# One load for x's tiles 4 to 15, a part of the output projection moved ahead, and score matmuls that share their weights

## The chip, the cores and the metric

The kernel runs on one core of one Trainium2 chip. A core has four engines that compute: TensorE (PE in the profile; its weight loads are listed apart as PEld), VectorE (DVE), ScalarE (ACT) and GpSimd (POOL). SyncE (SP) issues most of the transfers, which 16 DMA engines carry out. Each engine runs its own instructions in order and waits on semaphores for the others. The metric is the device time of one execution in microseconds, as the median of several runs.

## The reference: what is computed

A transformer block for 2048 positions of width 640, with a modulation that depends on a vector c.

```
sa, ca, ga, sb, cb, gb = six rows of  silu(c) @ w_mod
h  = layernorm(x) * (1 + ca) + sa
q  = h @ wq                                  (32 heads of width 128)
p  = softmax(q @ k_cache^T * 128 ** -0.5)     (2048 keys per head)
x  = x + ga * ((p @ v_cache) @ wo)
h  = layernorm(x) * (1 + cb) + sb
u  = gelu(layernorm(h) @ w1), its four column groups shifted by +1, -1, +2, -2 positions
x1 = h + u @ w2
B  = x1 + gelu(layernorm(x1) @ w3) @ w4       (inner width 1728)
out = x + gb * B
```

Tensors are bfloat16; matmuls accumulate in float32.

## The kernel before

Positions are worked in 16 tiles of 128 rows (NQT). A small class, Prog, takes every operation with the keys that it reads and writes, in the order in which the code calls for it, and puts a semaphore wait only where one engine must wait for another or for a transfer. There is no scheduler: the order of the calls is the order on each engine, and the order of the transfers on SP is the order of the calls as well. A transfer whose wait is not yet over holds back everything behind it on SP.

**The start** normalizes x, transposes it to hT, and computes the modulation rows.

**The loop** (L533) runs over 512 steps s, one for each head and tile (NG = 32 * 16), and then on for PVD + LAG = 12 steps that only finish what is under way. A step has two halves of 1024 keys. For each half TensorE computes the scores of tile s (qk, L279: two matmuls of 512 columns with the same QT slice as weights, L286), then half of the value products of the step eight before (pv, L292: eight matmuls of 129 columns, L299), then at most one piece of the next head's projection (q_piece, L237) or four transposes (t_piece, L253). VectorE negates and scales the scores and takes their minimum (L575). ScalarE takes the exponential (L588) into the slot s % 10 of a ring (Pb). Most tiles are then transposed by a DMA from Pb to the ring's second half (transpose, L220; the issue is L222), and two tiles in 16 by TensorE. GpSimd divides by the sums and stores the outputs to a scratch tensor in HBM (norm, L445; L454).

**Around the end of the loop**, SP is given, in this order: the outputs of tiles 0 and 1 as transposing loads in three parts (load_ot, L496, issue L497; parts of 12, 12 and 8 heads, the last at step NG), x's tiles 0 to 3 (load_xt(0), L503, issue L504), the outputs of tiles 2 and 3 (load_ot(1)), and at step NG + 2 x's tiles 4 to 7 (load_xt(1)). Outputs of even pairs go to a buffer in hTx, those of odd pairs to one in negS. The first tile's projection with wo (a_pe, L516, L525) is split: its first two parts stand between the last value products, at steps NG + 3 and NG + 4, and its third part behind the loop. A projection of a tile is 32 heads times two matmuls, of 512 and 128 columns, in one of two score banks that ybank hands out in turn.

**The first stretch behind the loop** (L719) takes tile after tile: a_pe(i) on TensorE; then a_s1 (L634), which multiplies by ga and adds x (L636, L638) and takes the statistics (L629, L631, and L622, L624 on GpSimd); a_s2 of the tile before (L642), which modulates (L644, L647) and takes statistics again; nrm_of (L652) of the tile before that, which normalizes (L654); and from i = 3 on the transposes n_t (L658; L663 on TensorE, L666 on ScalarE). In this stretch SP gets, at i = 1, the load of the third pair's outputs (load_ot(2), which waits until TensorE has read the first pair), then x's tiles 8 to 11 and 12 to 15, then w1 and w2.

**Where things lie.** xt (x again) and xb (the modulated rows) are placed in the memory of the ring, behind one another: xt begins at element 3072, xb at 3072 + 16 * 640 = 13312. Their transfers and writes take the keys of the ring slots of 2048 elements that they touch (ringk, L304). x's tiles 12 to 15 take slots 5 and 6; xb's tile 0, written by L647, takes slots 6 and 7. tmp, written by L636, takes slots 0 and 1; x's tiles 0 to 3 take slots 1 and 2.

**The second stretch** goes on with w1 (b_op, L698), w2 (c_op, L765), w3 (d_op, L780) and w4 (e_op, L829, and e_last, L812), mostly on TensorE.

Of the kernel before, what the change touches and what calls it, by code (L numbers as in the profile page):

```python
# [1 line left out]

# [4 lines left out]
ACT = mybir.ActivationFunctionType  # L7
BF16 = mybir.dt.bfloat16
F32 = mybir.dt.float32


class Prog:
# [103 lines left out]
def bass_adaLN_cond__mha_block_cached__mixer_s_mlp__prompt_kernel(  # L116
    nc, A_x, A_k_cache, A_v_cache, A_wq, A_wo, B_x, B_w1, B_w2, B_w3, B_w4, c, w_mod, out,
):
    _, SQ, D = A_x.shape
# [5 lines left out]
    NQC = SQ // 512  # L125
# [6 lines left out]
    NG = H * NQT  # L132
    x2d = A_x[0]
# [4 lines left out]
    with ExitStack() as es:  # L138
# [5 lines left out]
        Sps = ps("Sps", [128, 2048], F32)  # L144
# [5 lines left out]
        if True:  # L150
            with ExitStack() as es1:
                sb1 = lambda name, shape, dt: es1.enter_context(nc.sbuf_tensor(name, shape, dt))
                RP = 10
                PVD = 8
# [19 lines left out]
                KTs = kv[:, 0:o1].rearrange("p (b s) -> p b s", b=2)  # L174
                Vaug = kv[:, o1:o2].rearrange("p (b k d) -> p b k d", b=2, k=NKT)
                wq = kv[:, o2:o3].rearrange("p (b k d) -> p b k d", b=2, k=KT)
                QT = kv[:, o3:o3 + 2 * SQ].rearrange("p (b q) -> p b q", b=2)
# [101 lines left out]
                def qk(s, half):  # L279
                    h, j = divmod(s, NQT)  # L280
                    hb = h % 2

                    def f(t):
                        for c2 in range(2):
                            col = half * 1024 + c2 * 512
                            ins = t.matmul(Sps[:, col:col + 512], QT[:, hb, j * 128:(j + 1) * 128],  # L286
                                           KTs[:, hb, col:col + 512], start=True, stop=True)
                        return ins
                    G.op("tensor", f, r=[("QT", hb, j // 4), ("KT", hb)],
                         w=[("S", half)] + ([("Sb", 2 * half), ("Sb", 2 * half + 1)] if s == 0 else []))  # L290

                def pv(g, half):  # L292
# [11 lines left out]
                ringk = lambda a, b: [k for i in range(a // SK, -(-b // SK)) for k in (  # L304
                    [("Pb", i)] if i < RP else [("PT", i - RP, 0), ("PT", i - RP, 1)])]
# [153 lines left out]
                XT0 = 3072  # L459
# [40 lines left out]
                          w=[("OT", pr % 2, i) for i in ([part] if h1 - h0 < H else range(3))]  # L500
                          + ((HTK if pr == 0 else NEG) if pr < 2 else []))

                def load_xt(cc):  # L503
                    G.dma("sync", lambda e: e.dma_start(  # L504
                        xt[:, 4 * cc:4 * cc + 4], x2d[cc * 512:(cc + 1) * 512, :].rearrange("(t p) d -> p t d", p=128)),
                        ("xt", cc), w=[("x1", t) for t in range(4 * cc, 4 * cc + 4)]
                        + ringk(XT0 + 4 * cc * D, XT0 + 4 * (cc + 1) * D))

                OTC = [0, 12 * H // 32, 24 * H // 32, H]
                yn = [0]  # L510
# [22 lines left out]
                for s in range(NG + PVD + LAG):  # L533
                    h, j = divmod(s, NQT)
                    g_ = s - PVD
                    evacs = []
                    if s <= 2:
                        for i in ((0,), (1, 2), range(3, len(MROW)))[s]:
                            mod_rows(i)
                    if s == 3:  # L540
                        G.op("gpsimd", lambda g: g.tensor_scalar(
                            out=mod_bc[:, 2 * D:3 * D], in0=mod_bc[:, 2 * D:3 * D], scalar1=1.0, scalar2=1.0, op0=ALU.add, op1=ALU.mult),
                            r=[("mod", i) for i in range(len(MROW))], w=["mod"])
                    for half in range(2):
                        if s < NG:
                            qk(s, half)
                        if half == 0 and s in (NG + PVD - 5, NG + PVD - 4):
                            b0 = a_pe(0, None if s == NG + PVD - 5 else b0, (s - NG - PVD + 5,))
                        if 0 <= g_ < NG:
                            pv(g_, half)  # L550
                        if s == 0 and half == 1:
                            q_head0(NQC - 1)
                        if h + 1 < H and 2 * j + half in QPIECE:
                            cc, q = QPIECE[2 * j + half]
                            q_piece(h + 1, cc, q)
                            if q == KT - 1:
                                evacs.append((q_evac, h + 1, cc))
                        for r in range(2):
                            g = s - 3 - r
                            if 0 <= g < NG and is_pe(g):  # L560
                                t_piece(g, r, half)
                                if half == 1:
                                    evacs.append((t_evac, g, r))
                    if 0 <= g_ < NG and g_ % 2 == 1:
                        p = g_ // 2
                        G.op("scalar", lambda a, p=p: a.copy(  # L566
                            Of[:, p % 4].rearrange("p z d -> p (z d)")[:, 0:259], PO[:, (p % 2) * 512:(p % 2) * 512 + 259]),
                            r=[("O", p % 2)], w=[("Of", p % 4)])
                    for fn, x, y in evacs:
                        if fn is q_evac or not by_dve(x, y):  # L570
                            fn(x, y)
                    for half in range(2):
                        if s < NG:
                            r8 = s % 8
                            G.op("vector", lambda v, half=half, s=s, r8=r8: v.tensor_scalar(  # L575
                                out=negS[:, s % 3, half * 1024:(half + 1) * 1024],
                                in0=Sps[:, half * 1024:(half + 1) * 1024],
                                scalar1=-SCALE, scalar2=None, op0=ALU.mult, op1=ALU.min,
                                accum_out=(nm0 if half == 0 else nm1)[:, r8:r8 + 1]),
                                r=[("S", half)], w=[("negS", s % 3), ("nmh", half, r8)])  # L580
                    for fn, x, y in evacs:
                        if fn is t_evac and by_dve(x, y):
                            fn(x, y)
                    if s < NG:
                        G.op("gpsimd", lambda g, r8=r8: g.tensor_scalar(  # L585
                            out=nm[:, r8:r8 + 1], in0=nm0[:, r8:r8 + 1], scalar1=nm1[:, r8:r8 + 1], scalar2=None, op0=ALU.min),
                            r=[("nmh", 0, r8), ("nmh", 1, r8)], w=[("nm", r8)])
                        G.op("scalar", lambda a, s=s, r8=r8: a.activation(  # L588
                            Pb[:, s % RP, :], negS[:, s % 3, :], ACT.Exp, bias=nm[:, r8:r8 + 1], scale=-1.0),
                            r=[("negS", s % 3), ("nm", r8)], w=[("Pb", s % RP)])  # L590
                        if not is_pe(s):
                            if s % 2 == 1 and not is_pe(s - 1):
                                transpose(s - 1, 2)
                            elif s % 2 == 1 or is_pe(s + 1):
                                transpose(s, 1)
                        if j == 2 and h >= 1 and h + 1 < H:
                            load_k(h + 1)
                        if h + 1 == H and j in (2, PVD + 1):
                            i = 0 if j == 2 else 1
                            load_ot(0, OTC[i], OTC[i + 1], i)  # L600
                        if j == 6 and h + 2 < H:
                            load_wq(h + 2)
                        if j == PVD + 1 and h + 1 < H:
                            load_v(h + 1)
                    if 0 <= s - PVD - LAG:
                        gr, z = divmod(s - PVD - LAG, 4)
                        if z == 0:
                            rcp(gr)
                        norm(gr, z)
                    if s == NG:  # L610
                        G.op("gpsimd", lambda g: g.memset(mhalf, -0.5), w=["mhalf"] + NEG)
                        load_ot(0, OTC[2], OTC[3], 2)
                        load_xt(0)
                        load_ot(1)
                    if s == NG + 2:
                        load_xt(1)
                GELU = ACT.Gelu_apprx_tanh
                NB = [PTp[:, 0:1024], PTp[:, 1024:2048]]
                TMPK = ringk(0, 4 * D)
# [52 lines left out]
                for n in range(KT):  # L672
                    lst = []
                    p = 0
                    while p < 128:
# [8 lines left out]
                        p = pe_  # L684
# [33 lines left out]

                for i in range(NQT):  # L719
                    if i < NQT - 2:  # L720
                        b = a_pe(0, b0, (2,)) if i == 0 else a_pe(i)
                        if i >= 3:
                            n_t(i - 3, i == 3)
                    if i == NQT - 3:
# [2 lines left out]
                    if i % 2 == 1 and (i + 3) // 2 < NQT // 2:  # L727
                        load_ot((i + 3) // 2)
                    if i == 1:
                        for cc in range(2, NQC):  # L730
                            load_xt(cc)
                        G.dma("sync", lambda e: e.dma_start(w1, B_w1.rearrange("(k p) n -> p k n", p=128)), "w1", w=["w1"] + KVK)
                        G.dma("sync", lambda e: e.dma_start(w2, B_w2.rearrange("(k p) n -> p k n", p=128)), "w2", w=["w2"] + NEG)
                    if i < NQT - 2:
# [166 lines left out]
```

## Time and profile before

| | us |
|---|---|
| median of 3 runs | 1607.3 |
| lowest and highest run | 1603.85, 1612.64 |
| the profiled execution | 1608.8 |
| its span, first to last instruction | 1607.0 |
| mean granted TensorE clock in it | 0.994 |
| score pass on VectorE (L575), 1024 of 1220 ns | 1179.0 |
| exponentials on ScalarE (L588), 512 of 2017 ns | 1028.3 |
| value products on TensorE (L299), 8192 matmuls | 646.5 |
| score matmuls (L286), 2048 | 614.8 |
| weight loads of the score matmuls (L286), 2048 of 97 ns | 144.8 |

The page gives, for each group of instructions, the busy time and the mean of one, and behind a bar the time in which the engine stood idle just before them, with what ended most of that idle time. The matmuls are pipelined and their ends are modelled, so for TensorE the starts tell more than the durations. A row in order of time has start, duration, engine and line, what is written and read, and in brackets the idle time ahead of it with its releaser. In a row of windows, the three numbers at the end are the granted TensorE clock, the DMA share and GB/s.

### The profile page before, as it was taken

How to read it: one execution, taken by the hardware profiler on the slowest of the kernel's cores; microseconds unless marked ns; L12 is line 12 of the kernel's file. 1: busy time of each engine (PE TensorE's matmuls, PEld its weight loads, DVE VectorE, ACT ScalarE, POOL GpSimd, SP SyncE). 2: the span in 40 equal slices, each digit the busy share in tenths (PEclk: the TensorE clock that was granted, in tenths of full speed). 3: DMA queues.
4: the chain of work that ended last, by engine and by line, in shares of the span. 5: the costliest groups of instructions: out<-in, count | busy, mean ns of one | idle time of the engine just before them, and what ended most of it. 6: DMA issues, size and time to landing. Idle time of an engine off the chain costs nothing.

```text
span 1607.0 us, 34876 instructions
## 1 busy us (share of the span) xinstructions
PE 1502.1 (93%) x14231; PEld 965.9 (60%) x14231; DVE 1395.2 (87%) x2463; ACT 1296.4 (81%) x1145; POOL 624.7 (39%) x1396
## 2 busy tenths in 40 slices
PE   5899999999999999989999999999999879999999
PEld 3466666666666666666666666666666645555555
DVE  6999999999999999999999999999999546666435
ACT  4999999999999999999999999999999600035331
POOL 0244444444444444444444444444444423323100
PEclk9999999999999999999999999999999989999999
DMA  9999999999999999999999999999999993603000
GB/s 308 232 223 239 230 239 239 228 243 245 236 241 245 236 240 239 235 231 230 234 247 239 240 231 237 235 247 228 244 226 243 235 265 68 142 3 111 9 25 34
DMA packets 1167936, 333.60 MB, mean 208 GB/s; under 512 B 1148384, under 2 KB 1161760, under 8 KB 1167776
## 3 DMA queue, kind: packets, MB, share of 16 engines
q1 hardware_dynamic: 1161632, 314.59, 97.8%
q0 software_dynamic: 6144, 16.79, 3.6%
q8 instruction: 112, 1.84, 0.5%
q14 instruction: 48, 0.39, 0.1%
HBM read 43.48 MB, written 19.40 MB: 39 GB/s over the span
## 4 chain that ended last, share of the span: by engine, by line
DVE 30%; ACT 24%; PE 21%; DMA 15%; issue 8%; POOL 1%; SPq 1%; POOLq 0%; DVEq 0%
DVE negS L575 27%; ACT ring L588 19%; DMA ring<-ring 14%; PE Sps L525 7%; PE Sps L829 4%; ACT ring L262 2%; PE QPp L780 2%; PE Oaug L780 2%; PE Sps L765 1%; PE PTp L299 1%; ACT Of L566 1%; ACT kv L244 1%; DVE ring L264 1%; PE Sps L286 1%; DMA ring<-in_A_x_dram 1%
## 5 line engine op out<-in xcount | busy, mean ns | idle before, releaser
L575 DVE TENSOR_SCALAR_CACHE_REDUCE negS<-Sps 128x1024 f32<-128x1024 f32 x1024 | 1179.0, 1220 | 39.0 <-PE Sps L286 38.9
L588 ACT ACTIVATE ring<-negS,small 128x2048 bf16<-128x2048 f32 x512 | 1028.3, 2017 | 26.2 <-POOL small L585 24.7
L299 PEld LDWEIGHTS PTp<-kv,ring 128*128 128x128 bf16 x8192 | 551.4, 98 | 317.0 <-DMA ring<-ring 102.2
L299 PE MATMUL PTp<-kv,ring 128*128 128x129 bf16 x8192 | 646.5, 221 | 55.5 <-DMA ring<-ring 54.7
L286 PE MATMUL Sps<-kv 128*128 128x512 bf16 x2048 | 614.8, 382 | 18.8 <-DVE negS L575 13.4
L585 POOL TENSOR_SCALAR small<-small 128x1 f32<-128x1 f32 x512 | 147.1, 287 | 637.1 <-DVE negS L575 637.0
L286 PEld LDWEIGHTS Sps<-kv 128*128 128x128 bf16 x2048 | 144.8, 97 | 139.5 <-DVE negS L575 93.4
L447 POOL TENSOR_SCALAR On<-Of,small 128x128 bf16<-128x128 f32 x512 | 191.5, 374 | 13.0
L440 POOL TENSOR_TENSOR small<-Of,small 128x4 f32<-128x4 f32 x128 | 133.3, 1042 | 8.2 <-ACT Of L566 8.2
L666 ACT COPY kv<-PTp 128x640 bf16<-128x640 bf16 x32 | 22.0, 692 | 137.1 <-PE PTp L663 137.1
L237 PE MATMUL Oaug<-hTx,kv 128*128 128x512 bf16 x320 | 121.0, 382 | 2.4 <-ACT hTx L391 1.5
L237 PE MATMUL QPp<-hTx,kv 128*128 128x512 bf16 x320 | 120.3, 380 | 2.3 <-ACT hTx L391 1.6
L454 POOL DMA_DIRECT2D o_scratch<-On x128 | 103.1, 806 | 40.8 <-POOL On L447 37.2
L566 ACT COPY Of<-PTp 128x259 f32<-128x259 f32 x256 | 95.8, 374 | 13.4 <-PE PTp L299 13.4
L575 DVE DVE_READ_ACCUMULATOR negS<-Sps 128x1 f32 x1024 | 85.3, 83 | 0.0
L622 POOL TENSOR_SCALAR negS<-negS 128x1 f32<-128x1 f32 x48 | 24.7, 515 | 147.7 <-DVE negS L631 147.6
L525 PE MATMUL Sps<-wo,hTx 128*128 128x128 bf16 (+1 forms) x512 | 72.9, 303 | 0.0
L525 PE MATMUL Sps<-wo,negS 128*128 128x128 bf16 (+1 forms) x512 | 71.7, 299 | 0.4 <-DMA negS<-o_scratch 0.4
L636 DVE TENSOR_TENSOR ring<-Sps,mod_bc 128x640 f32<-128x640 f32 x16 | 13.1, 821 | 63.5 <-PE Sps L525 42.7
L262 ACT COPY ring<-Oaug 128x1024 bf16<-128x1024 bf16 x64 | 65.1, 1018 | 2.5 <-PE Oaug L253 2.5
L833 DVE TENSOR_TENSOR ring<-Sps,ring 128x640 f32<-128x640 f32 x15 | 12.4, 824 | 58.5 <-PE Sps L829 58.5
L525 PEld LDWEIGHTS Sps<-wo,negS 128*128 128x128 bf16 x512 | 40.1, 98 | 32.5 <-DMA negS<-o_scratch 0.6
(90 smaller groups left out, 1010.4 us busy)
## 6 DMA issues: line engine op xcount, KB each, us to landing
kv<-in_A_v_cache_dram SPq DMA_DIRECT2D x32, 512.0 KB, 5.1
o_scratch<-On POOLq DMA_DIRECT2D x128, 128.0 KB, 4.0
ring<-in_A_x_dram SPq DMA_DIRECT2D x8, 640.0 KB, 5.4
kv<-in_A_wq_dram SPq DMA_DIRECT2D x32, 160.0 KB, 3.3
wo<-in_A_wo_dram SPq DMA_DIRECT2D x1, 5120.0 KB, 16.8
ring<-ring SPq DMA_TRANSPOSE x256, 7.2
ring<-in_w_mod_dram SPq DMA_DIRECT2D x1, 3200.0 KB, 12.9
out_dram<-wo SPq DMA_DIRECT2D x15, 160.0 KB, 1.8
```

The lines of the kernel that those rows point to most:

```text
L237: G.op("tensor", lambda t: t.matmul(JB[jb], wq[:, hb, q, :], hT[:, q, cc * 512:(cc + 1) * 512], start=(q == 0), stop=(q == KT - 1)), r=[(" ...
L262: G.op("scalar", lambda a: a.copy(dst, src), r=[("J", jb)], w=[("PT", g % RP, r)])
L286: ins = t.matmul(Sps[:, col:col + 512], QT[:, hb, j * 128:(j + 1) * 128], KTs[:, hb, col:col + 512], start=True, stop=True)
L299: ins = t.matmul(ob[:, 0:129], PTs[:, b, kt, :], Vaug[:, hb, kt, 0:129], start=(kt == 0), stop=(kt == NKT - 1))
L440: G.op("gpsimd", lambda g: g.tensor_tensor(out=rl[:, 4 * b:4 * b + 4], in0=Of[:].rearrange("p a z d -> p (a z) d")[:, 4 * b:4 * b + 4, 128 ...
L447: G.op("gpsimd", lambda g: g.tensor_scalar(out=On[:, b, z, :], in0=Of[:, 2 * b + z // 2, z % 2, 0:128], scalar1=rl[:, 4 * b + z:4 * b + z ...
L454: G.dma("gpsimd", lambda e: e.dma_start(o_scr[jj // 2:jj // 2 + 2, :, hh].rearrange("a p z d -> p a (z d)"), On[:, b].rearrange("p (a z) d ...
L525: ins = t.matmul(YB[b][:, c0:c0 + cw], OTj[pr % 2][:, 2 * hh + z, :], wo[:, hh, c0:c0 + cw], start=(hh == 0), stop=(hh == H - 1))
L566: G.op("scalar", lambda a, p=p: a.copy(Of[:, p % 4].rearrange("p z d -> p (z d)")[:, 0:259], PO[:, (p % 2) * 512:(p % 2) * 512 + 259]), r= ...
L575: G.op("vector", lambda v, half=half, s=s, r8=r8: v.tensor_scalar(out=negS[:, s % 3, half * 1024:(half + 1) * 1024], in0=Sps[:, half * 102 ...
L585: G.op("gpsimd", lambda g, r8=r8: g.tensor_scalar(out=nm[:, r8:r8 + 1], in0=nm0[:, r8:r8 + 1], scalar1=nm1[:, r8:r8 + 1], scalar2=None, op ...
L588: G.op("scalar", lambda a, s=s, r8=r8: a.activation(Pb[:, s % RP, :], negS[:, s % 3, :], ACT.Exp, bias=nm[:, r8:r8 + 1], scale=-1.0), r=[( ...
```

## The change

Four edits:

1. A helper emits a matmul that has no weight load of its own. The second of the two score matmuls of each half (L286) uses it.
2. load_xt takes a first and a last group of four tiles. At step NG + 2 one transfer brings x's tiles 4 to 15, in place of tiles 4 to 7; the two transfers at i = 1 go.
3. So w1 and w2 follow directly on the third pair's outputs.
4. The first 12 heads of the second tile's projection are computed at step NG + PVD - 2, ahead of the value products of the last two steps; behind the loop the other 20 heads follow.

```
+def same_weights(t, out, lhsT, rhs, start, stop):
+    return t.add_instruction(mybir.InstMatmult(
+        name=t.bass.get_next_instruction_name(), ins=[t.lower_ap(rhs), t.lower_ap(lhsT)], outs=[t.lower_ap(out)],
+        start_tensor_calc=start, stop_tensor_calc=stop, ldweights=False, tile_position=(0, 0), tile_size=(128, 128)))
...
-                            ins = t.matmul(Sps[:, col:col + 512], QT[:, hb, j * 128:(j + 1) * 128],
-                                           KTs[:, hb, col:col + 512], start=True, stop=True)
+                            ins = (t.matmul if c2 == 0 else partial(same_weights, t))(
+                                Sps[:, col:col + 512], QT[:, hb, j * 128:(j + 1) * 128], KTs[:, hb, col:col + 512], start=True, stop=True)
...
-                def load_xt(cc):
+                def load_xt(c0, c1):
                     G.dma("sync", lambda e: e.dma_start(
-                        xt[:, 4 * cc:4 * cc + 4], x2d[cc * 512:(cc + 1) * 512, :].rearrange("(t p) d -> p t d", p=128)),
-                        ("xt", cc), w=[("x1", t) for t in range(4 * cc, 4 * cc + 4)]
-                        + ringk(XT0 + 4 * cc * D, XT0 + 4 * (cc + 1) * D))
+                        xt[:, 4 * c0:4 * c1], x2d[c0 * 512:c1 * 512, :].rearrange("(t p) d -> p t d", p=128)),
+                        ("xt", c0), w=[("x1", t) for t in range(4 * c0, 4 * c1)] + ringk(XT0 + 4 * c0 * D, XT0 + 4 * c1 * D))
...
+                        if half == 0 and s == NG + PVD - 2:
+                            b1 = a_pe(1, None, (0,))
                         if 0 <= g_ < NG:
                             pv(g_, half)
...
-                        load_xt(0)
+                        load_xt(0, 1)
                         load_ot(1)
                     if s == NG + 2:
-                        load_xt(1)
+                        load_xt(1, NQC)
...
-                        b = a_pe(0, b0, (2,)) if i == 0 else a_pe(i)
+                        b = a_pe(0, b0, (2,)) if i == 0 else a_pe(1, b1, (1, 2)) if i == 1 else a_pe(i)
...
                     if i == 1:
-                        for cc in range(2, NQC):
-                            load_xt(cc)
                         G.dma("sync", lambda e: e.dma_start(w1, B_w1.rearrange("(k p) n -> p k n", p=128)), "w1", w=["w1"] + KVK)
```

More of the change, by code (lines that the diff above doesn't have):

```diff
@@ L1 @@
 from contextlib import ExitStack
+from functools import partial
 import concourse.bass as bass
```

## The prediction

> **What bounds the kernel now.** I read the page's head and costliest groups first, then the list of waits, then the order of time in one stretch of the loop and in the stretch behind it. The page:
>
> ```profile
> span 1607.0 us, 34876 instructions
> PE 1502.1 (93%) x14231; PEld 965.9 (60%) x14231; DVE 1395.2 (87%) x2463; ACT 1296.4 (81%) x1145; POOL 624.7 (39%) x1396
> ...
> L575 DVE TENSOR_SCALAR_CACHE_REDUCE negS<-Sps 128x1024 f32<-128x1024 f32 x1024 | 1179.0, 1220 | 39.0 <-PE Sps L286 38.9
> ...
> L286 PE MATMUL Sps<-kv 128*128 128x512 bf16 x2048 | 614.8, 382 | 18.8 <-DVE negS L575 13.4
> ...
> L286 PEld LDWEIGHTS Sps<-kv 128*128 128x128 bf16 x2048 | 144.8, 97 | 139.5 <-DVE negS L575 93.4
> ```
>
> VectorE's score pass (L575) is busy 1179 us and stood idle 39 us in front. The list of waits of the whole run says what starved it: TensorE itself waits for transposes of the probabilities.
>
> ```profile
> PE PTp L299 <- DMA ring<-ring: 54.7, 69, 2.4
> DVE negS L575 <- PE Sps L286: 38.9, 54, 2.7
> ```
>
> Inside the loop, in order of time (start, duration, engine, line):
>
> ```profile
> 905.34 0.61 PE L286 MATMUL Sps<-kv 128*128 128x512 bf16 x2
> 905.78 0.63 PE L299 MATMUL PTp<-kv,ring 128*128 128x129 bf16 x8
> 906.25 0.38 PE L237 MATMUL Oaug<-hTx,kv 128*128 128x512 bf16 x1
> 906.48 0.60 PE L286 MATMUL Sps<-kv 128*128 128x512 bf16 x2
> ...
> 905.56 0.67 PEld L299 LDWEIGHTS PTp<-kv,ring 128*128 128x128 bf16 x8
> ```
>
> Starts are to be read, not durations: two score matmuls take 905.34 to 905.78, 0.44 us or 0.22 each; eight value products 0.47 or 0.059 each; one projection piece 0.23. The half step is 1.14 us on TensorE, and VectorE's half is as long (1.145 from start to start in the unstalled loop). Loads lie beside matmuls: eight in 0.67 us while eight products pass.
>
> Behind the loop:
>
> ```profile
> 1283.86 10.87 SPq L497 DMA_TRANSPOSE negS<-o_scratch  x1
> 1294.78 0.58 SPq L504 DMA_DIRECT2D ring<-in_A_x_dram  x1
> 1296.57 8.80 SPq L497 DMA_TRANSPOSE hTx<-o_scratch  x1
> 1296.89 17.56 PE L525 MATMUL Sps<-wo,negS 128*128 128x512 bf16 x128 [0.40 <-DMA negS<-o_scratch]
> 1305.41 5.28 SPq L504 DMA_DIRECT2D ring<-in_A_x_dram  x2
> 1314.71 0.89 DVE L647 SCALAR_TENSOR_TENSOR ring<-ring,negS,mod_bc 128x640 f32<-128x640 f32 x1 [14.59 <-DMA ring<-in_A_x_dram]
> 1322.84 0.71 PE L663 MATMUL PTp<-ident,Of 128*128 128x128 bf16 x5 [8.40 <-DVE Of L654]
> 1323.35 10.77 PE L525 MATMUL Sps<-wo,hTx 128*128 128x512 bf16 x64
> 1334.24 8.86 PE L525 MATMUL Sps<-wo,hTx 128*128 128x512 bf16 x64
> ```
>
> VectorE waits 14.59 us for an x load that the first row does not use: xb's tile 0 begins in ring slot 6, where x's tiles 12 to 15 end, and the dependency is kept by slot. That load is the second of the x2 at 1305.41; it stands on SP behind the third outputs' load and waits for tiles 8 to 11. TensorE then waits 8.40 us for the first normalized tile, and comes back slow: 64 projections take 10.77 us where the next 64 take 8.86. The windows show the clock:
>
> ```profile
> 1129.20:1132.60 3.40, 3.40 (x27) 2.78 (x26) 1.23 (x2) 0.97 (x1) 0.00 (x0) 0.51 1.28 289
> ...
> 1322.84:1327.20 4.36, 4.36 (x15) 1.88 (x16) 4.22 (x7) 0.69 (x1) 2.04 (x3) 0.50 0.89 201
> ```
>
> (The number third from the right is the granted clock.) From 1330 us to the end the chain is TensorE alone, and its waits in that stretch add up to under 1 us: what TensorE gains by 1323, the end gains.
>
> **The change, part by part.** *x in one load.* Two issues (0.58 and 0.37 us) and SP's wait of 4.3 us between them go; one issue of 1920 KB stands where 640 KB were issued, at 1294.78. Issue to landing was 9.3 us for 2160 KB and 8.2 for 2080 KB (w3 and w4), so I take 8.5: x lands at 1303.3. Between the first reader, L647 at 1314.71, and the end of the first L654 at 1322.8 lie 8.1 us of VectorE work, so the first normalized tile could be ready at 1311.4; but the third tile's projection ends only 8.7 us after 1296.89, at 1305.6, and from there six us of VectorE work are left (0.82 + 0.82 + 0.89 + 0.21 of the sum and its statistics, 0.83 + 0.89 + 0.89 + 0.21 of the second tile's modulation, 0.56): 1311.7. TensorE arrives at 1314.45. The 8.40 us go whole, with 2.7 us in hand. The slow return goes as well: 10.77 - 8.86 = 1.91, and 0.71 - 0.44 = 0.27 for the five transposes. Sum 10.6 us.
>
> What is queued behind it on SP: the third outputs' load. It landed at 1308.9, 9.5 us after the x load before it (1299.4); behind an x load that lands at 1303.3 it lands at 1312.8, and the tile that reads it is due on TensorE at 1314.7. Covered, by 2 us. w1 and w2 follow it about 5 us sooner than now; their readers begin at 1417. The fourth outputs' load waits for TensorE at 1314.45 as before. POOL's queue is not passed.
>
> *The wo part ahead of the last value products.* Its 24 matmuls are moved, not added: 12 of 512 columns by 0.216 and 12 of 128 by 0.056, 3.3 us. They read outputs that the first tile's part read at 1270.7 already, and a score bank that VectorE left at 1268.6, so they wait for nothing. They stand where TensorE idles 2.38 us for the last transposes (to 1283.47), so the last products, and the copies and stores behind them on ACT and POOL, come 0.9 us later; those stores are read by a load issued after 1379. The two first tiles end at 1296.5 - 3.3 + 0.9 = 1294.1. What is late next is the second outputs' load: SP issues it at 1283.86, after a wait for the last transposes that TensorE does not set, and it lands at 1296.84. TensorE waits 2.8 us there where it waited 0.40. The part alone gains nothing: the hole is moved.
>
> The moved hole has a price of its own. A hole of 2.12 us (1126.97 to 1129.09) was followed by 3.4 us at clock 0.51, the first windows row; the hole of 2.38 us at 1281 was followed by none. The new one is longer than both, so I take one slow stretch: half of 3.4 us, 1.7 us; bounds 0 and 1.7. [...]
>
> *Reused weights.* 1024 of 2048 score loads go, 97 ns each, 99 us of PEld. On the path I take 0. The loads removed stand behind a first matmul of 0.22 us that covers them. Where the first load has just been waited for, the two matmuls start 0.225 us apart, else 0.215: an exposed load shows as 10 ns. VectorE sets the pace beside it, and its idle 39 us follow late transposes. Bounds: the full 39 us gained; for a loss no row shows a matmul without its own load, and the nearest is one that waits for its predecessor to end, 382 - 216 = 166 ns. I take 0 since the nearest rows are the 10 ns and the back-to-back starts.
> [...]
>
> **Sum.** 10.6 - 1.7 + 0 + 0 = 8.9 us. The profiled execution took 1608.8 us (its span and 1.8 around it), which makes 1599.9; it lay 1.5 us above the median of the runs, 1607.3, so 1598.4 on their scale.
>
> **Rivals.** *No slow stretch*: 10.6 us, 1596.7. For it: the 2.38 us hole; against: the 2.12 us one.
> *x or the third outputs come late*: if 1920 KB need what the three loads need now (4.6 + 4.9 + 4.3 = 13.8 us), x lands at 1308.6, the normalized tile is ready at 1316.7 and the outputs at 1318.1. TensorE waits up to 3.4 us and gains 5.5 to 7.2: 1600 to 1602. Against: w3's 9.3 us.
> *Reuse frees the loop*: up to 39 us more, 1560. For it: VectorE's waits name TensorE. Against: TensorE's own waits behind them name the transposes.
> *The bare second matmul stalls* (the other side): 28 of 32 half steps of a head carry a projection piece or transposes and have no room, 896 in all. Each exposed 0.166 us costs 149 us: 1747. It is slower than now by 0.5% from about 20 ns per half step (17 us / 896). Nothing in the trace shows such a stall, and nothing shows that it can't be.
> That two of the three parts, the reuse and the wo part, do nothing for the time is in the forecast itself.
>
> **How the numbers follow.** Slow stretch 0.46, no slow stretch 0.24, late loads 0.10, loop freed 0.07, stall 0.13. 0.5% is 8 us, about what this kernel's measurement tells from no change (its runs spread over 8.8). The first case lies 0.9 us beyond that bound, so a part of it falls within 0.5%: faster 0.60, same 0.27, slower 0.13. Range 1590 to 1608: the first three cases with 3 to 7 us for the runs' spread, leaving out the loop freed and the stall. The likeliest case's own range is 1594 to 1603.
>
> **What would show it.** Right: L647 starts near 1303 to 1305 with a wait of a few us; the first L663 follows L525 without a hole; TensorE waits 2 to 3 us for negS<-o_scratch before the third tile, and 24 matmuls of L525 stand between value products; the score loads number 1024 and the loop's last L575 starts near 1267. Wrong: L575's idle time changed by over 10 us either way, pairs of score matmuls more than 0.24 us apart, or a new wait of TensorE for hTx<-o_scratch at the fifth tile.

## The result, and the profile after

The changed kernel takes 1595.6 us (median of 14 runs, 1592.4 to 1599.2) where the kernel before took 1605.3 beside it: a ratio of 0.9939 (95% interval 0.9924 to 0.9953), or 9.7 us less. Forecast were 8.9 us less.

The profiled execution took 1592.4 us, 16.4 less than the profiled execution of before. Medians differ by 9.7, so one pair of profiles must not be read as the gain. It splits in two at the start of the last score pass (L575 before, L584 after; the 35 us ahead of the first score pass are 0.5 us longer after):

| us | before | after |
|---|---|---|
| first to last score pass (the loop) | 1232.2 | 1223.8 |
| last score pass to the end (the tail) | 339.6 | 331.1 |
| of the tail, up to the first transposes of normalized tiles | 55.4 | 49.1 |

The tail is 8.5 us shorter, near the 8.9 that were forecast (7.7 us in a second pair of profiles, e9 and e10). The 8.4 us of the loop are looked into below (e1, e9 to e12).

The page after; lines have moved by 7 to 9, and the second score matmul of a pair has the helper's line, L15:

```profile
span 1590.6 us, 33595 instructions
...
L584 DVE TENSOR_SCALAR_CACHE_REDUCE negS<-Sps 128x1024 f32<-128x1024 f32 x1024 | 1178.6, 1220 | 30.9 <-PE Sps L15 30.5
...
L15 PE MATMUL Sps<-kv 128*128 128x512 bf16 x1024 | 387.9, 379 | 12.6 <-DVE negS L584 6.6
...
L294 PEld LDWEIGHTS Sps<-kv 128*128 128x128 bf16 x1024 | 98.3, 96 | 109.3 <-DVE negS L584 87.2
```

Half of the score loads are gone (1024 of 96 ns are left). VectorE's score pass is as long as before, 1220 ns, and stood idle 30.9 us in front, where it was 39.0. The list of waits names the same two:

```profile
PE PTp L307 <- DMA ring<-ring: 48.6, 71, 1.9
...
DVE negS L584 <- PE Sps L15: 30.5, 46, 2.2
```

The tail in order of time:

```profile
1276.25 11.56 SPq L505 DMA_TRANSPOSE negS<-o_scratch  x1
1287.91 0.53 SPq L512 DMA_DIRECT2D ring<-in_A_x_dram  x1
1288.54 15.27 SPq L505 DMA_TRANSPOSE hTx<-o_scratch  x1
1290.23 18.49 PE L532 MATMUL Sps<-wo,negS 128*128 128x512 bf16 x126 [4.12 <-DMA negS<-o_scratch]
1297.02 0.88 DVE L656 SCALAR_TENSOR_TENSOR ring<-ring,negS,mod_bc 128x640 f32<-128x640 f32 x1 [7.27 <-DMA ring<-in_A_x_dram]
1308.56 0.44 PE L672 MATMUL PTp<-ident,Of 128*128 128x128 bf16 x5
1309.05 8.64 PE L532 MATMUL Sps<-wo,hTx 128*128 128x512 bf16 x63
```

VectorE still waits for x (L656), 7.27 us, but TensorE does not feel it: the first transposes (L672) follow the projection with no hole, and the next projection runs at full pace. In exchange TensorE waits 4.12 us for the second outputs (0.40 before). The windows around that wait, the third number from the right being the granted clock:

```profile
1289.10:1290.20 1.10, 0.00 (x0) 0.13 (x2) 0.65 (x1) 0.00 (x0) 1.02 (x2) 0.52 0.80 120
1290.20:1292.50 2.30, 2.27 (x6) 0.89 (x6) 0.00 (x0) 0.00 (x0) 0.25 (x1) 0.50 0.96 328
```

The clock fell at 1289.1, while TensorE was still waiting, and stayed at half for 3.4 us.

### The profile page after: what moved, and what is told of

Same layout as the page of the kernel before. It is cut to its first block, busy times and chain, and to the rows that moved or that the text cites. A ratio compares the mean times of both kernels' runs of the same rounds, so it can differ in the third digit from the quotient of the medians.

```text
span 1590.6 us, 33595 instructions
## 1 busy us (share of the span) xinstructions
PE 1477.4 (93%) x13976; PEld 916.9 (58%) x13207; DVE 1395.0 (88%) x2463; ACT 1295.8 (81%) x1145; POOL 622.0 (39%) x1396
## 4 chain that ended last, share of the span: by engine, by line
DVE 34%; ACT 22%; PE 21%; DMA 13%; issue 9%; POOL 2%; SPq 0%; POOLq 0%; DVEq 0%
DVE negS L584 31%; ACT ring L597 18%; DMA ring<-ring 12%; PE Sps L532 8%; PE Sps L836 4%; ACT ring L270 2%; PE Oaug L787 2%; PE QPp L787 2%; PE Sps L772 1%; ACT kv L252 1%; ACT Of L575 1%; PE PTp L307 1%; DVE ring L272 1%; DMA negS<-o_scratch 1%; POOL small L594 1%
## 5 line engine op out<-in xcount | busy, mean ns | idle before, releaser
L584 DVE TENSOR_SCALAR_CACHE_REDUCE negS<-Sps 128x1024 f32<-128x1024 f32 x1024 | 1178.6, 1220 | 30.9 <-PE Sps L15 30.5
L307 PE MATMUL PTp<-kv,ring 128*128 128x129 bf16 x8192 | 645.7, 220 | 49.0 <-DMA ring<-ring 48.6
L15 PE MATMUL Sps<-kv 128*128 128x512 bf16 x1024 | 387.9, 379 | 12.6 <-DVE negS L584 6.6
L294 PE MATMUL Sps<-kv 128*128 128x512 bf16 x926 | 355.3, 384 | 21.9 <-DVE negS L584 10.8
L294 PEld LDWEIGHTS Sps<-kv 128*128 128x128 bf16 x1024 | 98.3, 96 | 109.3 <-DVE negS L584 87.2
L575 ACT COPY Of<-PTp 128x259 f32<-128x259 f32 x256 | 96.0, 375 | 14.3 <-PE PTp L307 14.3
L245 PE MATMUL Oaug<-hTx,kv 128*128 128x512 bf16 x264 | 100.4, 385 | 3.4 <-DVE hTx L404 3.4
L245 PE MATMUL QPp<-hTx,kv 128*128 128x512 bf16 x259 | 97.5, 381 | 2.4 <-ACT hTx L399 1.7
L584 DVE DVE_READ_ACCUMULATOR negS<-Sps 128x1 f32 x1024 | 84.9, 83 | 0.0
L532 PE MATMUL Sps<-wo,hTx 128*128 128x512 bf16 (+1 forms) x502 | 69.3, 297 | 0.5
```

Of the source, the lines that this page charges most:

```text
L15: return t.add_instruction(mybir.InstMatmult(name=t.bass.get_next_instruction_name(), ins=[t.lower_ap(rhs), t.lower_ap(lhsT)], outs=[t.low ...
L245: G.op("tensor", lambda t: t.matmul(JB[jb], wq[:, hb, q, :], hT[:, q, cc * 512:(cc + 1) * 512], start=(q == 0), stop=(q == KT - 1)), r=[(" ...
L294: ins = (t.matmul if c2 == 0 else partial(same_weights, t))(Sps[:, col:col + 512], QT[:, hb, j * 128:(j + 1) * 128], KTs[:, hb, col:col + ...
L307: ins = t.matmul(ob[:, 0:129], PTs[:, b, kt, :], Vaug[:, hb, kt, 0:129], start=(kt == 0), stop=(kt == NKT - 1))
L532: ins = t.matmul(YB[b][:, c0:c0 + cw], OTj[pr % 2][:, 2 * hh + z, :], wo[:, hh, c0:c0 + cw], start=(hh == 0), stop=(hh == H - 1))
L575: G.op("scalar", lambda a, p=p: a.copy(Of[:, p % 4].rearrange("p z d -> p (z d)")[:, 0:259], PO[:, (p % 2) * 512:(p % 2) * 512 + 259]), r= ...
```

## The experiments

The runs were measured in three groups, e1 to e4, e5 to e8 and e9 to e12, each with the kernel before beside it. Gains in us are worked out from the ratio. Loop and tail lengths come from each run's one profile. Two profiles of one kernel differed by 0.4 to 1.9 us in the tail (before and e9, the full change and e10, e7 and e12) and by up to 8.0 us in the loop (before and e9). So each run is told by its ratio to the kernel before and by its tail.

| | ratio to before | interval | loop, us | tail, us | last score pass to first transposes |
|---|---|---|---|---|---|
| e1 reuse alone | 0.9988 | 0.9978 to 0.9998 | 1223.4 | 341.7 | 57.4 |
| e2 x load alone | 0.9934 | 0.9918 to 0.9949 | 1221.8 | 330.4 | 48.3 |
| e3 wo part alone | 0.9990 | 0.9980 to 1.0001 | 1225.4 | 341.2 | 56.4 |
| e4 x load and wo part | 0.9936 | 0.9916 to 0.9956 | 1220.9 | 332.8 | 50.8 |
| e5 key | 0.9919 | 0.9905 to 0.9933 | 1225.2 | 330.2 | 48.2 |
| e6 full change, load split | 0.9910 | 0.9895 to 0.9925 | 1221.4 | 330.6 | 48.6 |
| e7 key, wo part, split, reuse | 0.9865 | 0.9848 to 0.9881 | 1223.0 | 326.2 | 43.9 |
| e8 full change, reuse in the projection | 0.9901 | 0.9884 to 0.9919 | 1221.4 | 332.2 | 50.2 |
| e9 the kernel before | 0.9990 | 0.9974 to 1.0006 | 1224.2 | 340.7 | 56.6 |
| e10 the full change again | 0.9922 | 0.9901 to 0.9943 | 1222.9 | 333.0 | 51.0 |
| e11 as e7, without reuse | 0.9911 | 0.9889 to 0.9934 | 1227.5 | 326.6 | 44.0 |
| e12 e7 again | 0.9884 | 0.9860 to 0.9907 | 1219.8 | 326.6 | 44.6 |

### e1 to e4: the parts apart

e1 is the second score matmul without its load, and nothing else:

```
-  ins = t.matmul(Sps[:, col:col + 512], QT[...], KTs[...], start=True, stop=True)
+  ins = (t.matmul if c2 == 0 else partial(same_weights, t))(Sps[:, col:col + 512], QT[...], KTs[...], start=True, stop=True)
```

> Only the reused score weights. Theory (loads were hidden, the reuse is worth nothing): the same time as before, within 2 us; score matmuls of a pair still start 0.215 or 0.225 us apart; the loop, from the first to the last L575, stays at about 1232 us. Rival (the reuse frees the loop; the two profiled loops were 1232.2 and 1223.8 us long): 4 to 9 us faster, and TensorE arrives at the score matmuls earlier.

Measured: 1.9 us less, at the edge of what the theory allows, and far from the 8 us by which the two first profiles differed in the loop. The medians, 1602.0 and 1602.2, differ by 0.2 us, and e9 shows 1.6 us for no change at all. Pairs of score matmuls still start 0.215 or 0.225 us apart. The loop took 1223.4 us, where the theory expected 1232; e9 shows a loop of that kind without any edit. The holes behind the loop are all still there (VectorE's 14.4 us wait for x among them). More on this at e9 to e12.

e2 is the x load alone:

```
-  load_xt(1)            (at step NG + 2)
+  load_xt(1, NQC)
...
-  for cc in range(2, NQC): load_xt(cc)      (at i = 1)
```

> Only the one x load. Theory: the hole of 8.4 us ahead of the first transposes of normalized tiles goes, and the slow clock behind it; no hole is moved, so the wait for the second outputs' load stays near 0.4 us: 10.6 us faster, 0.9934 of before. From the last L575 to the first of those transposes 55.4 - 8.4 = 47.0 us. Rival (the x load is hidden anyway and the gain came from the loop): same time as before.

Measured: 0.9934, 10.6 us by that ratio, the forecast figure of this part; the medians, 1593.0 and 1602.2, differ by 9.2. TensorE in order of time:

```profile
1273.84 3.04 PE L299 MATMUL PTp<-kv,ring 128*128 128x129 bf16 x32 [2.65 <-DMA ring<-ring]
1277.10 11.27 PE L524 MATMUL Sps<-wo,hTx 128*128 128x512 bf16 x79 [0.22 <-issue]
1288.42 17.33 PE L524 MATMUL Sps<-wo,negS 128*128 128x512 bf16 x126
1305.59 0.44 PE L662 MATMUL PTp<-ident,Of 128*128 128x128 bf16 x5
```

No wait for the second outputs, none ahead of the first transposes. The hole ahead of the last value products (2.65 us) was followed by a slow clock here, which the profile of before did not show at the same place: 32 products took 3.04 us where 2.04 is the usual. It cost about 1.4 us: the second outputs had landed at 1286.94, and TensorE came to them at 1288.42. The first transposes stand 48.3 us behind the last score pass, where 47.0 were expected.

e3 is the wo part alone:

```
+  if half == 0 and s == NG + PVD - 2: b1 = a_pe(1, None, (0,))
...
-  b = a_pe(0, b0, (2,)) if i == 0 else a_pe(i)
+  b = a_pe(0, b0, (2,)) if i == 0 else a_pe(1, b1, (1, 2)) if i == 1 else a_pe(i)
```

> Only the wo part ahead. Theory: the hole is moved to the second outputs' load (0.4 becomes 3 to 4 us), and VectorE's wait for x still sets the first transposes: 0 us, within 2. Rival (3.3 us of TensorE work in a hole is 3.3 us gained): 3 us faster.

Measured: 0.9990, whose interval holds 1, and a tail of 341.2 us. The waits behind the loop show the hole at its new place, and VectorE's wait for x where it was:

```profile
DVE ring L649 <- DMA ring<-in_A_x_dram: 16.9, 1, 16.9
...
PE PTp L665 <- DVE Of L656: 6.0, 1, 6.0
...
PE Sps L525 <- DMA negS<-o_scratch: 3.7, 1, 3.7
```

What was taken out of one hole came back as 3.7 us of another. Alone the part is worth nothing that can be told.

e4 has both edits, and no reuse.

> The x load and the wo part, score weights loaded each time. Theory: what the full change gives, 9 us faster (0.994), and 1 to 2 us slower than the x load alone, through the slow clock behind the moved hole. Rival (the reuse carries a part): 4 to 9 us slower than the full change.

Measured: 0.9936, the same as e2 within the intervals; the tail is 2.4 us longer than e2's in the profiles (332.8 and 330.4), through a wait of 4.6 us for the second outputs and a slower stretch behind it (from the third tile's start to the first transposes 1.7 us more than in e7). The theory's 9 us hold (10.3 by the ratio); against e2 it expected 1 to 2 us, which is too small for the times to tell. The rival, 4 to 9 us slower than the full change, is out: the full change gave 0.9939, and 0.9922 in e10.

### e5: the wait without the load

Does the x load have to be early, or did L647 only wait for a neighbour in its ring slot? The loads stay where they were; the slot's key is taken by L636, which the code calls for before the late x loads.

```
-  w=[("tmp", u)] + (TMPK if j < 2 else []))
+  w=[("tmp", u)] + (TMPK if j < 2 else []) + (ringk(XB0, XB0 + 2 * D) if j == 0 else []))
...
-  w=[("xb", j)] + ringk(XB0 + 2 * j * D, XB0 + 2 * (j + 1) * D))
+  w=[("xb", j)] + (ringk(XB0 + 2 * j * D, XB0 + 2 * (j + 1) * D) if j > 0 else []))
```

> The loads as before; only the slot's key is taken by the first tile's sum (L636), ahead of the x loads, so that the first modulated row (L647) waits for no load. Theory (the 8.4 us hole is a false dependence between neighbours in a ring slot, not a late x): the hole goes although x's last tiles land as late as before, at about 47 us behind the last score pass; 10.6 us faster, 0.9934, as with the x load alone. Rival (the gain needs the transfers to be out of the way sooner): 0 to 5 us faster.

Measured: 0.9919, 13.0 us where 10.6 were expected, and the first transposes 48.2 us behind the last score pass, as with the x load alone. The tail is 9.4 us shorter than in the first profile of before and 10.5 shorter than in e9. Three engines in order of time:

```profile
1293.82 0.89 DVE L647 SCALAR_TENSOR_TENSOR ring<-ring,negS,mod_bc 128x640 f32<-128x640 f32 x1
...
1299.99 5.26 SPq L504 DMA_DIRECT2D ring<-in_A_x_dram  x2
...
1308.76 0.44 PE L663 MATMUL PTp<-ident,Of 128*128 128x128 bf16 x5
```

L647 runs 6 us before SP even issues the last x loads, whose data land 48.5 us behind the last score pass (47.2 before). The data were not late; a key shared by neighbours was. The earlier load is one way to hide it, the key another.

### e6 and e7: the moved hole taken away

The second pair's outputs come in three parts, as the first pair's do, and the third tile's projection is cut to match.

```
-  + ((HTK if pr == 0 else NEG) if pr < 2 else []))
+  + ((HTK if pr == 0 else NEG if part == 0 else []) if pr < 2 else []))
...
-  load_ot(1)
+  for i in range(3): load_ot(1, OTC[i], OTC[i + 1], i)
...
+  def a_parts(j):
+      b = None
+      for i in range(3): b = a_pe(j, b, (i,))
+      return b
...
-  else a_pe(i)
+  else a_parts(i) if i == 2 else a_pe(i)
```

e6 is the full change with this.

> The full change, and the second outputs' load cut into parts of 12, 12 and 8 heads, the third tile's projection with it. Theory (the wo part only moved its hole to this load): TensorE's 4.3 us wait at the third tile falls below 1 us and the slow clock there goes; VectorE's x then lands 2 us too late, so of about 5.5 us some 3 are left: 0.992 of before. Rival (the transposing load delivers no part before about its end): as the full change, 0.994, with the wait of about 4 us as it was.

The third tile starts after 0.65 us of waiting and runs at full pace (17.33 us, where the full change took 18.49), and the gain is given back two tiles later:

```profile
1284.10 17.33 PE L532 MATMUL Sps<-wo,negS 128*128 128x512 bf16 x126 [0.65 <-DMA negS<-o_scratch]
1305.33 0.45 PE L673 MATMUL PTp<-ident,Of 128*128 128x128 bf16 x5 [3.89 <-DVE Of L664]
```

x now comes too late: VectorE waits 10.11 us for it at L657. Of the 4.4 us that TensorE had gained on the full change by then it loses 3.89; the tail is 330.6 us, 0.5 less than the full change in the first profile and 2.4 less than in e10. The ratio, 0.9910, is near the 0.992 expected. The loss is larger than the 2 us expected: x lands 40.4 us after the last score pass (37.4 with the full change), since its load is issued 1.6 us later, behind three parts, and is 1.3 us longer under way.

e7 puts e5's key in the place of the x load, and keeps the wo part, the split and the reuse.

> Key as in e5, wo part ahead, second outputs' load in three parts, reused score weights; x loads where they were before. Theory (both holes gone at once): first transposes of normalized tiles about 44 us behind the last score pass where it was 55.4 before and 49.1 with the full change; 13.6 us faster than before, 0.9915, or 4 us faster than the full change. Rival (the tail is bound by something else, such as the outputs' loads): no faster than the full change, 0.994.

Both holes are gone:

```profile
1277.39 7.55 PE L533 MATMUL Sps<-wo,hTx 128*128 128x512 bf16 x55
1284.99 17.33 PE L533 MATMUL Sps<-wo,negS 128*128 128x512 bf16 x126
1302.16 0.44 PE L674 MATMUL PTp<-ident,Of 128*128 128x128 bf16 x5
```

The first transposes stand 43.9 us behind the last score pass, where 44 were expected, and the tail is 326.2 us, 13.4 less than in the first profile of before. The time is 1583.0 us against 1605.4 (0.9865): 22.4 us, some 9 us more than the tail explains. The repeat, e12, gave 0.9884. It is the fastest version here and beats the full change, in e10 and e12 by 1593.5 to 1587.6.

### e8: reuse where TensorE sets the pace

In the loop VectorE hid what TensorE saved (e1: 1024 loads of 97 ns fewer, 1.9 us less). In the projection TensorE alone sets the pace (after: tile follows tile every 8.97 us with no wait), and each head's weights serve two column groups.

```
-  for c0, cw in NC2:
-      for hh in range(h0, h1):
-          ins = t.matmul(...)
+  for hh in range(h0, h1):
+      for c0, cw in NC2:
+          ins = (t.matmul if c0 == 0 else partial(same_weights, t))(...)
```

> The full change, and the projection with wo takes its two column groups head by head, the second (128 columns) without a weight load of its own: 512 loads fewer in a stretch where TensorE alone sets the pace. Theory (loads are hidden, so their number is nothing): 8.69 us for a tile as now, the same time as the full change. Rival (loads cost time on the path): up to 0.03 us for each of the 512, 15 us faster. Other side (a load is taken no further ahead than one matmul, and 98 ns do not fit behind a bare matmul of 56 ns): up to 0.04 us for each head, 1.3 us for a tile, 20 us slower.

```profile
1300.19 0.38 PE L532 MATMUL Sps<-wo,negS 128*128 128x512 bf16 x1
1300.40 0.22 PE L15 MATMUL Sps<-wo,negS 128*128 128x128 bf16 x1
1300.46 0.38 PE L532 MATMUL Sps<-wo,negS 128*128 128x512 bf16 x1
```

A head takes 0.272 us (1300.19 to 1300.46), and from tile to tile it is 8.97 us, to the hundredth as with all loads. The theory holds in the tail (332.2 us). The ratio, 0.9901, is below the full change's 0.9939 and 0.9922; the loop, which this edit does not touch, is where profiles of one kernel differ too.

### e9 to e12: what the loop does by itself

These are the kernel before against itself, the full change again, and e7 without and with reuse.

> The kernel before, unchanged, measured as if it were a variant: what these comparisons show for no change. Theory (they are true to 0.2%): 1.000, within 0.002, the loop from the first to the last L575 between 1221 and 1232 us in its profile, as in the other profiles, and 339 to 342 us behind it. Rival (the loops of the variants, 1221 to 1225 us, were shortened by their edits; before's is 1232): a loop of about 1232 us again.

> The full change once more, beside e9, e11 and e12. Theory (its gain is the 8.5 us behind the loop): 0.994 to 0.995. Rival (the last call's ratios, some 3 us lower than the tails explain, are gains in the loop): 0.991.

> e7 with a weight load for every score matmul. Theory (the reuse is worth nothing): e12's time within 2 us. Rival (the reuse shortens the loop, 1219 us for e7 by its median less its tail): 3 to 5 us slower than e12.

> e7 once more. Theory (13.4 us less behind the loop): 0.9917 of before. Rival: 0.9865 as e7 showed, 22 us, of which 9 would lie in the loop.

e9: 0.9990, with a loop of 1224.2 us. So the 1232.2 us in the first profile of before were one long loop, and for the most part not what the edits shortened; the comparisons are off by 0.1% here. e10: 0.9922, between the theory's 0.994 to 0.995 and the rival's 0.991; its interval holds both 0.994 and 0.991, so it does not decide. e11 and e12 differ by 4.2 us (1591.8 and 1587.6; runs of 1587.6 to 1594.7 and 1583.2 to 1588.6, which overlap by 1 us): the rival's figure, not the theory's. The interval of e12 leaves out its theory's 0.9917. Their tails are equal, 326.6 us; the difference is in the loop, 1227.5 and 1219.8 us in the profiles. The list of waits of e11 and then of e12:

```profile
PE PTp L299 <- DMA ring<-ring: 50.8, 72, 1.7
...
DVE negS L577 <- PE Sps L286: 33.3, 49, 2.2
```

```profile
PE PTp L307 <- DMA ring<-ring: 43.8, 63, 1.7
...
DVE negS L585 <- PE Sps L15: 27.4, 42, 2.2
```

With reuse, TensorE finds a transpose late less often here (63 and 72 times). Over all profiles the two groups overlap: 61 to 71 times in the seven with reuse, 67 to 72 in the seven without. The loops are 1219.8 to 1223.8 us long with reuse and 1220.9 to 1232.2 without (means 1222.2 and 1225.3). TensorE's own work is not what got shorter: the shortest half steps with a projection piece take 1.11 us in both groups, those with four transposes 1.12, those with neither 0.90. The transposes, from issue to landing, take 6.80 to 6.84 us on the mean of a profile with reuse and 6.83 to 6.89 without.

One more reading of the same runs takes from each gain what the tail explains, measured against e9's tail of 340.7 us. In each of the three groups the versions with reuse have more left (e1 2.9 us; e6 to e8 4.3 to 7.4; e10 and e12 4.8 and 4.5) than those without (e2 to e4 0.3 to 2.4; e5 2.5; e9 and e11 1.6 and 0.2). The first result has 0.2 us left and does not show it, and e4 and the full change, which differ by the reuse alone, gave nearly the same ratio. So the reuse may be worth 2 to 4 us in the loop; this is not shown beyond the spread of the loops. That it would come through transposes that are late less often is a guess from the means above. Why they should land sooner when TensorE loads fewer weights is open; no run varied it.

## Why the prediction was right

*x in one load: right.* It was priced at 10.6 us, and alone it gave 0.9934 of before, 10.6 us. That the two agree to a tenth is luck: by the medians the gain is 9.2 us, by the tails 9.2 (before) or 10.3 (e9), and a slow clock of 1.4 us that the price did not have lies in it. The mechanism is shown by e5: the wait was kept by the ring slot, not by the data. The load took 9.0 us from issue to landing (forecast 8.5, from w3 and w4), and the chain of VectorE that was worked out row by row ended 2.3 us before TensorE needed it (forecast 2.7). The third outputs' load landed 46.3 us behind the last score pass, where 45.4 were expected, and no one waited for it. One detail was wrong and cost nothing: w1 and w2 were to come about 5 us sooner, but w1 was issued at 44.4 us, where it had been at 43.3, behind an issue of the third outputs that took 15.27 us on SP in place of 8.80.

*The wo part: right that it gains nothing and only moves the hole.* The wait at its new place was 4.1 us, not 2.8. TensorE reached it when it was expected (26.7 us behind the last score pass, as forecast); the second outputs landed later, at 30.3 where they had at 29.4. That load ends 29.4 to 31.7 us behind the last score pass in these profiles with no part of it changed.

*The slow clock behind the moved hole: right that it comes; its size was luck.* 1.7 us were taken, as the upper bound; 126 projection matmuls took 18.49 us and in e7, without the hole, 17.33: 1.2 us. A third of the slow stretch ran out while TensorE still waited. From the third tile's start to the first transposes it was 1.7 us more than in e7 in e4, 1.8 in e8 and 3.2 in e10. So the bound was too low, and why more was lost in e10 is open. A hole of 2.65 us in e2 was followed by a slow stretch as well (32 products in 3.04 us, where 2.04 is the usual), and one of 2.38 us in the profile of before was not (32 products in 2.04 us; more on this in the last section). Such a hole was there without the wo part too, so to charge the slow clock to the wo part alone was too simple; e4 and e2 differ by less than the times can tell.

*Reuse at 0: right on TensorE, perhaps 2 to 4 us too low in the loop (not shown).* The shortest half steps (1.11 us with a projection piece, with and without reuse) and e8's tiles (8.97 us, as with all loads) say that here a load behind a matmul cost nothing, and that a matmul without a load cost nothing either, so the rival that a bare matmul stalls is out. In e8 that is 512 loads of 98 ns fewer, and not a hundredth of a microsecond per tile. What the forecast had not thought of is a possible effect past TensorE, on how often transposes are late.

*The sum* was 8.9 us; the tails of the two first profiles differ by 8.5, the medians by 9.7. In the tail two misses partly cancel: the second outputs landed 0.9 us later than before, and the slow clock cost 0.5 us less than it was charged. What would have gone wrong had the profiles been compared by themselves is the loop: 8.4 us of their difference are mostly the spread of one kernel from run to run.

## What to carry to other kernels

Before a transfer is moved, ask what the waiting instruction needs: here it read none of the data, and a narrower key gave the same gain with every load in its old place. Work put into a hole gains only if what the engine waits for next does not come at its own time (e3: a wait of 0.40 us became one of 3.7); follow the chain one wait further, and mend that wait (a load in parts) in the same change. And split a pair of profiles at a fixed point before a gain of half a percent is explained: the loop, in which the forecast saw no gain, differed by as much as the tail.

## What was not expected of the hardware

In e8 a weight load recorded as 98 ns stood ahead of a matmul that started 56 ns after the one before it, and delayed nothing: heads took 0.216 + 0.056 us with one load each, and tiles 8.97 us, as with two. So the load's recorded duration was not the time that the path needed. A loop with the same instructions took 1232.2 and 1224.2 us in two profiles of one kernel.

The length of a hole on TensorE did not tell whether the clock fell behind it. Holes of 2.12 us (before, in the loop: clock 0.51 from 1129.20 to 1132.60) and 2.65 us (e2: 32 products in 3.04 us, where 2.04 is the usual) were followed by a slow stretch; one of 2.38 us (before: clock 1.00 from 1282.90 to 1286.30) and one of 3.89 us (e6: five transposes in 0.45 us, where 0.44 is the usual) were not.

The profiles of before and after tell when the clock fell to half: in before at 23.33, 30.16, 1129.25 and 1316.98 us, in after at 22.80, 29.63, 1289.14 and 1589.52 us. From one start to the next it is 6.83, 1099.09 and 187.73 us in before, 2, 322 and 55 times 3.413, and 6.83, 1259.52 and 300.37 us in after, 2, 369 and 88 times. So within each of the two profiles the starts fit a grid of 3.413 us. Leave out the first 60 and the last 25 us: then TensorE had been idle for 62% (before, 1125.83 to 1129.25), 74% (before, 1313.57 to 1316.98) and 89% (after, 1285.73 to 1289.14) of the grid step ahead of the three slow stretches in that range. Of the other steps at full clock none was idle for more than 55% (before, 682.10 to 685.51). In before the hole of 2.38 us lay across two steps, the first idle for 51% (1279.43 to 1282.84). This is read from the two traces; no run moved a hole against the grid.
